# Router weights loaded third, value halves made with the keys', no sum begun where another ended, three row buffers, limits of one element

## The chip, the cores and the metric

The kernel runs on one core of a Trainium2 chip. The metric is the device time of one execution in microseconds. The engines are named as in the profile: PE (TensorE: matmuls; PEld its weight loads), DVE (VectorE), ACT (ScalarE), POOL (GpSimd) and SP (SyncE, which here issues the DMAs); a trailing q (SPq) is an engine's instruction queue. Each engine works through its own instructions in order and waits for the others by semaphores.

## What is computed

Thresholded attention over 2 batches, 8 heads, 576 positions and 64 elements a head (in each row of scores only those within tau of the row's maximum stay), then a feed-forward layer (512 to 2048 to 512, ELU), then a mixture of 8 experts, each token to its best one:

```python
scores = scale * q @ k.T
thresh = max(scores, axis=-1) - tau
scores = where(scores >= thresh, scores, -1e9)
attn = exp(scores - max(scores)); attn /= attn.sum(-1)
x = (attn @ v) as [1152 tokens, 512]
h = x @ w_in;  x = where(h > 0, h, exp(min(h, 0)) - 1) @ w_out
logits = x @ w_gate;  e = argmax(logits)        # at most 288 tokens for each expert
out = softmax(logits)[e] * (relu(x @ w1[e]) @ w2[e])
```

## The kernel before

The 1152 tokens make 9 tiles of 128. Operands of matmuls are split into two fp16 halves (a high one, and a low one made of the rest), and a product is three matmuls.

The first part is written out by hand, in steps i = 0 to 37 (`manual_schedule`): the order of the lines is each engine's order. A step is one pair of heads (j = i % 4) of one query tile (t = i // 4). The two score tiles of a step are already computed by PE at the end of the step before. In a step, in this order: PE multiplies the probabilities of step i - 2 with the values (`emit_pv`); SP issues loads (`load_k`, `load_v`, `load_q`); while keys are still to be prepared (i = 0 to 2 and 15 to 18), ACT copies the next pair's keys to fp16 (`prep_k`, first half, L216); `emit_max` takes on DVE both heads' maxima (L272) and then the two limits, nb for the exponential (L273) and th for the mask (L274), each as one instruction on two elements per partition; ACT makes both exponentials (L278); DVE makes the keys' low half (L218). In steps 0 to 16 conversions of the feed-forward weights follow (`conv`: three DVE instructions, L363, L364, L367, then two on ACT and one on POOL), one here and, from step 2 on, one more at the end of the step. DVE then masks each head with its sum (L284), PE computes the next step's scores (L250), ACT copies the probabilities to fp16 (L293), POOL makes their low half (L294) and SP transposes them by DMA (L299, tile pt). The end of the step holds `setup_rest` (in step 0), the values' halves (`prep_v`: ACT L107, DVE L108; steps 0 to 3 and 16 to 19), the q halves of the next tile (j = 2) and, in steps 14 to 19, one sixth each of the zero fill of the DRAM table disp (L180). `zero_out` writes zeros to the output in step 26.

Feed-forward work is put into the steps by `piece`, from step 7 on: three calls in steps 7 to 17 (FILL = 3), two afterwards. All but the last stand before the masks, as piece(2), and take only second-layer products (`mm2_chunk`, L423, 12 matmuls); the last stands at the end of the step, as piece(1), and takes a first-layer chunk (`mm1_chunk`, L391, 48 matmuls) where one is ready. Second-layer products of a tile are summed in one PSUM bank, mmb (one buffer). A sum of two products is emptied by ACT (L434, `acc`) and later added to by DVE (L437); a sum that ends at the fourth product starts the tile's routing. The emptying is written by `settle`, after the masks and the scores. What is left of the pieces when the steps are over runs in a loop of single pieces, whose instructions are not in an order written out by hand.

`route` copies a finished tile's row to a row buffer x2 (ACT L447 high half, DVE L452 low half; two buffers), transposes it by DMA, takes logits on PE, chooses and ranks on DVE, one tile at a time and a piece of it per step, and sends the rows into disp by an indirect DMA from POOL (L503). After the loop the last tile is routed; the transposed rows of expert 0 (xa, L596) are read for that. The experts follow, with weights loaded in 32 parts (stg).

## Time and profile before

| | us |
|---|---|
| runs of the kernel before | 601.43, 598.35, 595.74; median 598.35 |
| the profiled execution | 600.27 |
| its span, first to last instruction | 598.6 |
| busy: PE, DVE, ACT, POOL | 447.4 (75%), 415.7 (69%), 350.4 (59%), 268.6 (45%) |
| mean granted clock of PE, share of full speed | 0.912 |
| the steps (first to last maximum) | 10.3 to 357.5 |

All times of single instructions are from the one profiled execution, counted from its span's start. A busy share is a mean over parts with different limits. Where the profile names what an engine waited for, it is the last of its semaphores by the profile.

### The profile page before, as it was taken

What the parts mean: (1) busy time and instruction counts of PE and PEld (TensorE: products, weight loads), DVE (VectorE), ACT (ScalarE), POOL (GpSimd) and SP (SyncE); (2) the same over time, 40 slices, a digit from 0 to 9 for tenths busy, and PEclk for the clock granted to TensorE, in tenths of its full rate; (3) what the DMA queues carried; (4) which work ended last, traced back from release to release, by engine and by line L of the source; (5) the groups of instructions that cost most, each with busy time, mean ns of one, the idle gap of its engine ahead of it and who ended that gap; (6) DMA issues with size and microseconds to landing.
All of it is one profiled execution on the core that took longest, in us unless ns stands there. A gap on an engine that the chain in (4) does not pass through costs nothing.

```text
span 598.6 us, 13017 instructions
## 1 busy us (share of the span) xinstructions
PE 447.4 (75%) x5343; PEld 361.3 (60%) x5343; DVE 415.7 (69%) x768; ACT 350.4 (59%) x511; POOL 268.6 (45%) x195
## 2 busy tenths in 40 slices
PE   1124255855848799679799999998799998788792
PEld 0013134534616477547477776777789998787671
DVE  4488899999968868578888874687336566655530
ACT  4346568677765765355667554677266675665531
POOL 0326466765764353536356553432432541442242
PEclk9997667879979899979999999998899999798897
DMA  5645677678786858625765444777377998797621
GB/s 180 209 138 146 180 203 212 192 199 229 174 202 184 169 130 220 116 55 119 200 184 111 86 93 99 206 286 240 111 146 246 275 234 257 250 260 217 202 60 38
DMA packets 150771, 105.59 MB, mean 176 GB/s; under 512 B 135209, under 2 KB 135209, under 8 KB 146608
## 3 DMA queue, kind: packets, MB, share of 16 engines
q1 hardware_dynamic: 148064, 99.94, 63.1%
q0 software_dynamic: 2640, 4.74, 2.2%
q8 instruction: 44, 0.72, 0.5%
q14 instruction: 23, 0.19, 0.1%
HBM read 60.06 MB, written 12.68 MB: 122 GB/s over the span
## 4 chain that ended last, share of the span: by engine, by line
DVE 39%; DMA 21%; issue 12%; ACT 12%; PE 12%; POOL 2%; SPq 1%; DVEq 0%; POOLq 0%; ACTq 0%
DMA stg<-in_w_dram 9%; DVE m L272 6%; DVE pp L284 6%; PE mma L391 4%; DVE we L639 4%; PE mmb L423 4%; DMA yr<-yt 4%; DVE cvp L364 4%; DVE cvp L363 3%; ACT pp L278 3%; DMA out_dram<-y,ix 3%; ACT we L636 2%; DVE gf L408 2%; DVE nb L273 2%; DMA disp<-x,slot_i 2%
## 5 line engine op out<-in xcount | busy, mean ns | idle before, releaser
L250 PE MATMUL s<-kst,qst 128*128 128x288 f16 (+1 forms) x320 | 54.1, 330 | 91.6 <-DVE pp L284 82.1
L294 POOL TENSOR_TENSOR phl<-pp,phl 128x1152 f16<-128x1152 f32 x36 | 85.5, 2374 | 81.7 <-issue 73.7
L423 PE MATMUL mmb<-wo,g 128*128 128x512 f16 x384 | 96.3, 402 | 20.9 <-ACT acc L434 7.9
L391 PEld LDWEIGHTS <-wi 128*128 128x128 f16 x1728 | 103.5, 101 | 9.7 <-issue 6.9
L639 DVE SCALAR_TENSOR_TENSOR we<-stg,we 128x1024 f16<-128x1024 f32 x64 | 79.5, 1276 | 37.8 <-ACT we L636 37.5
L250 PEld LDWEIGHTS <-qst 128*128 128x128 f16 (+1 forms) x320 | 28.9, 110 | 115.0 <-DVE pp L284 68.3
L278 ACT ACTIVATE pp<-s,nb,escale 128x576 f32<-128x576 f32 x72 | 55.9, 826 | 66.7 <-DVE nb L273 56.7
L391 PE MATMUL mma<-xt,wi 128*128 128x128 f16 x1392 | 87.2, 225 | 4.7 <-DVE gf L408 4.6
L636 ACT ACTIVATE we<-stg 128x1024 f16<-128x1024 f32 x64 | 64.2, 1047 | 42.5 <-DMA stg<-in_w_dram 41.6
L676 PE MATMUL mm<-xs,we 128*128 128x196 f16 x768 | 73.9, 261 | 13.3 <-DVE g L759 5.0
L676 PEld LDWEIGHTS <-we 128*128 128x128 f16 x768 | 70.3, 104 | 15.8 <-DVE we L639 8.0
L423 PEld LDWEIGHTS <-g 128*128 128x128 f16 x384 | 37.0, 102 | 66.4 <-issue 29.5
L689 POOL TENSOR_TENSOR ht<-rf,ht 128x392 f16<-128x392 f32 x32 | 35.2, 1109 | 77.1 <-ACT ht L688 40.0
L284 DVE SCALAR_TENSOR_TENSOR pp<-s,th,pp 128x576 f32<-128x576 f32 x72 | 55.9, 814 | 11.0 <-ACT pp L278 10.2
L413 POOL TENSOR_TENSOR g<-gf,g 128x512 f16<-128x512 f32 x36 | 45.1, 1254 | 34.4 <-ACT g L412 34.3
L732 PE MATMUL mm<-ht,we 128*128 128x196 f16 x672 | 58.4, 248 | 1.6 <-DVE yt L743 1.6
L732 PEld LDWEIGHTS <-we 128*128 128x128 f16 x672 | 57.4, 98 | 1.8 <-issue 1.7
L272 DVE TENSOR_REDUCE m<-s 128x1 f32<-128x576 f32 x72 | 50.9, 747 | 6.4 <-PE s L250 6.4
L293 ACT ACTIVATE phl<-pp 128x1152 f16<-128x1152 f32 x36 | 41.7, 1157 | 8.4 <-DVE pp L284 8.3
L316 PE MATMUL pv<-vst,pt 128*128 128x64 f16 (+3 forms) x1080 | 45.0, 204 | 1.9 <-DVE xf L332 1.9
L316 PEld LDWEIGHTS <-pt 128*128 128x128 f16 (+1 forms) x1080 | 42.8, 106 | 3.8 <-issue 2.3
L376 POOL TENSOR_TENSOR wi<-cv,wi 128x512 f16<-128x512 f32 x16 | 18.5, 1158 | 55.1 <-ACT cv L375 55.1
(128 smaller groups left out, 635.7 us busy)
## 6 DMA issues: line engine op xcount, KB each, us to landing
stg<-in_w_dram SPq DMA_DIRECT2D x32, 1024.0 KB, 5.2
cst<-in_w_in_dram SPq DMA_DIRECT2D x16, 512.0 KB, 4.3
cst<-in_w_out_dram SPq DMA_DIRECT2D x16, 512.0 KB, 4.2
disp<-zero SPq DMA_DIRECT2D x6, 771.0 KB, 6.8
qraw<-in_qt_dram SPq DMA_DIRECT2D x9, 512.0 KB, 4.6
vraw<-in_vb_dram SPq DMA_DIRECT2D x8, 320.0 KB, 5.9
kraw<-in_kt_dram SPq DMA_DIRECT2D x8, 288.0 KB, 6.5
out_dram<-zero SPq DMA_DIRECT2D x1, 2304.0 KB
```

The costliest lines, as they stand in the source:

```text
L250: nc.tensor.matmul(s[a:z, half, 0:288], q2[:, pas, h, a:z], kst[b, h // 2][:, h % 2, half * 288:(half + 1) * 288], start=(pas == 0), stop= ...
L272: nc.vector.tensor_reduce(out=m[:, z:z + 1], in_=sc[z], axis=AX.XY, op=ALU.max)
L278: nc.scalar.activation(out=pp[:, z].rearrange("p (a c) -> p a c", a=2), in_=s, func=ACTF.Exp, bias=nb[:, z:z + 1], scale=escale,)
L284: nc.vector.scalar_tensor_tensor(out=e, in0=s, scalar=th[:, z:z + 1], in1=e, op0=ALU.is_ge, op1=ALU.mult, accum_out=rsum[t_][:, h:h + 1],)
L294: nc.gpsimd.tensor_tensor(out=d[:, 1], in0=flat, in1=d[:, 0], op=ALU.subtract)
L316: nc.tensor.matmul(o[a:e, h:h + w // D, :].rearrange("p h d -> p (h d)"), q[:, ph * 9 + blk, a:e], vt[:, vh, c:c + w], start=(blk == 4 and ...
L391: nc.tensor.matmul(ps[:, o * P:(o + 1) * P], w[:, wh, kk, :], xt[t_][:, xh * 4 + kk, :], start=(k_ == 0), stop=(k_ == 11),)
L423: nc.tensor.matmul(ps, gt[t_, q][:, gh, o, :], w[:, wh, :], start=(first and o == 0 and n == 0), stop=(last_ and o == QF - 1 and n == 2),)
L636: nc.scalar.activation(out=w[:, 0, part], in_=t[:, part], func=ACTF.Copy, scale=SC)
L639: nc.vector.scalar_tensor_tensor(out=w[:, 1, part], in0=t[:, part], scalar=SC, in1=w[:, 0, part], op0=ALU.mult, op1=ALU.subtract)
L676: nc.tensor.matmul(ps[:, o * n:(o + 1) * n], w[:, wh, kk % 2, f * P:(f + 1) * P], t[:, xh * 4 + kk, :], start=(k_ == 0), stop=(k_ == 11),)
L732: nc.tensor.matmul(ps[:, o * n:(o + 1) * n], w[:, wh, f % 4, j * P:(j + 1) * P], h2[:, gh, f, :], start=(f == 0 and n_ == 0), stop=(f == 7 ...
```

## The change

- The load of the router weights goes out third, after the first k and q loads. The set-up instructions of POOL stand at the very start (`setup_pool`); what is left of `setup_rest` runs at the end of step 1 instead of step 0.
- `prep_v` becomes a generator like `prep_k`: its ACT copy stands before the maxima and exponentials of the step, its DVE low half after the keys' low half, before the conversion.
- `emit_max` works on one head: maximum, nb, and then the exponential of that head; the th limits of both heads follow. m, nb and th are tiles of one element per partition (four small instructions a step in place of two).
- `pick2` returns nothing while a sum has ended that `settle` has not yet emptied.
- Three row buffers x2 instead of two.
- The zero parts run in steps 8 to 13; the zero tile has half a row (514 elements), so that the transfers' pieces are half as long and twice as many (1,028 B instead of 2,056 B for disp, 1,024 B instead of 2,048 B for the output).

```diff
--- before.py
+++ after.py
@@ -67,7 +67,7 @@
     QF = 4
     QG = 2
 
-    ZSTEP, ZPARTS, ZOUT = 14, 6, 26
+    ZSTEP, ZPARTS, ZOUT = 8, 6, 26
     zeroed = [False]
 
     cap = min(cap, NT)
@@ -134,7 +134,7 @@
     cum = const.tile([P, E], F16, name="cum")
     wg_f = const.tile([P, 4, E], F32, name="wg_f")
     wg = const.tile([P, 2, 4, E], F16, name="wg")
-    zero = const.tile([P, ROW], F16, name="zero")
+    zero = const.tile([P, ROW // 2], F16, name="zero")
     lnsc = const.tile([P, 1], F32, name="lnsc")
     eps = const.tile([P, 1], F32, name="eps")
     xsc = const.tile([P, 1], F32, name="xsc")
@@ -151,41 +151,42 @@
             out=cadd, in0=neg, scalar=-3.0e38, in1=cadd, op0=ALU.mult, op1=ALU.add
         )
 
-    def setup_rest():
-        nc.sync.dma_start(out=wg_f, in_=w_gate)
-        nc.scalar.activation(out=wg[:, 0], in_=wg_f, func=ACTF.Copy, scale=SC)
-        nc.vector.scalar_tensor_tensor(
-            out=wg[:, 1], in0=wg_f, scalar=SC, in1=wg[:, 0], op0=ALU.mult, op1=ALU.subtract
+    def setup_pool():
+        nc.gpsimd.iota(ev_i, pattern=[[1, E]], base=-E, channel_multiplier=0)
+        nc.gpsimd.iota(ids, pattern=[[P, NTILE]], base=0, channel_multiplier=1)
+        nc.gpsimd.memset(ones, 1.0)
+
+        nc.gpsimd.affine_select(
+            out=tri, in_=ones, pattern=[[1, P]], compare_op=ALU.is_gt, fill=0.0,
+            base=0, channel_multiplier=-1,
         )
         nc.gpsimd.memset(lnsc, LN_GS)
         nc.gpsimd.memset(eps, 1e-9)
         nc.gpsimd.memset(xsc, SC / XS)
         nc.gpsimd.memset(zero, 0.0)
         nc.gpsimd.memset(cum, 0.0)
-        nc.gpsimd.memset(ones, 1.0)
-        nc.gpsimd.iota(ev_i, pattern=[[1, E]], base=-E, channel_multiplier=0)
+
+    def setup_rest():
+        nc.scalar.activation(out=wg[:, 0], in_=wg_f, func=ACTF.Copy, scale=SC)
+        nc.vector.scalar_tensor_tensor(
+            out=wg[:, 1], in0=wg_f, scalar=SC, in1=wg[:, 0], op0=ALU.mult, op1=ALU.subtract
+        )
         nc.vector.tensor_copy(ev, ev_i)
-        nc.gpsimd.iota(ids, pattern=[[P, NTILE]], base=0, channel_multiplier=1)
         nc.vector.tensor_scalar(ids, ids, OOB_ID, None, ALU.bitwise_xor)
-
-        nc.gpsimd.affine_select(
-            out=tri, in_=ones, pattern=[[1, P]], compare_op=ALU.is_gt, fill=0.0,
-            base=0, channel_multiplier=-1,
-        )
 
     def zero_fill(part, parts):
         n = E * CS // P
         r0, r1 = part * n // parts, (part + 1) * n // parts
         if r0 < r1:
             nc.sync.dma_start(
-                out=disp.rearrange("(p r) c -> p r c", p=P)[:, r0:r1],
-                in_=zero.bitcast(U16).unsqueeze(1).to_broadcast([P, r1 - r0, ROW]),
+                out=disp.rearrange("(p r) (a c) -> p (r a) c", p=P, a=2)[:, 2 * r0:2 * r1],
+                in_=zero.bitcast(U16).unsqueeze(1).to_broadcast([P, 2 * (r1 - r0), ROW // 2]),
             )
 
     def zero_out():
         nc.sync.dma_start(
-            out=out.rearrange("(p r) c -> p r c", p=P),
-            in_=zero[:, 0:2 * DM].bitcast(F32).unsqueeze(1).to_broadcast([P, NTILE, DM]),
+            out=out.rearrange("(p r) (a c) -> p (r a) c", p=P, a=2),
+            in_=zero[:, 0:DM].bitcast(F32).unsqueeze(1).to_broadcast([P, 2 * NTILE, DM // 2]),
         )
 
 
@@ -223,7 +224,11 @@
     def prep_v(b, j):
         v1 = raw_t.pop(("v", b, j))
         vt = attn.tile([P, 2, VC], F16, name="vst", tag="vst", bufs=6)
-        split(vt[:, 0], vt[:, 1], v1, SC, "dve")
+        nc.scalar.activation(out=vt[:, 0], in_=v1, func=ACTF.Copy, scale=SC)
+        yield
+        nc.vector.scalar_tensor_tensor(
+            out=vt[:, 1], in0=v1, scalar=SC, in1=vt[:, 0], op0=ALU.mult, op1=ALU.subtract
+        )
         vst[b, j] = vt
 
     def prep_q(t_):
@@ -263,26 +268,27 @@
     pv_ps = {}
     xt = {}
 
-    def emit_max(sc):
-
-        m = attn.tile([P, 2], F32, name="m", tag="m")
-        nb = attn.tile([P, 2], F32, name="nb", tag="nb")
-        th = attn.tile([P, 2], F32, name="th", tag="th")
-        for z in range(2):
-            nc.vector.tensor_reduce(out=m[:, z:z + 1], in_=sc[z], axis=AX.XY, op=ALU.max)
+    def emit_max(s):
+        m = attn.tile([P, 1], F32, name="m", tag="m", bufs=2)
+        nb = attn.tile([P, 1], F32, name="nb", tag="nb", bufs=2)
+        nc.vector.tensor_reduce(out=m, in_=s, axis=AX.XY, op=ALU.max)
         nc.vector.tensor_scalar(nb, m, cmul, None, ALU.mult)
+        return m, nb
+
+    def emit_thr(m):
+        th = attn.tile([P, 1], F32, name="th", tag="th", bufs=2)
         nc.vector.tensor_scalar(th, m, cadd, None, ALU.add)
-        return nb, th
+        return th
 
     def emit_exp(s, nb, pp, z):
         nc.scalar.activation(
-            out=pp[:, z].rearrange("p (a c) -> p a c", a=2), in_=s, func=ACTF.Exp, bias=nb[:, z:z + 1], scale=escale,
+            out=pp[:, z].rearrange("p (a c) -> p a c", a=2), in_=s, func=ACTF.Exp, bias=nb, scale=escale,
         )
 
     def emit_mask(s, th, pp, z, t_, h):
         e = pp[:, z].rearrange("p (a c) -> p a c", a=2)
         nc.vector.scalar_tensor_tensor(
-            out=e, in0=s, scalar=th[:, z:z + 1], in1=e, op0=ALU.is_ge, op1=ALU.mult,
+            out=e, in0=s, scalar=th, in1=e, op0=ALU.is_ge, op1=ALU.mult,
             accum_out=rsum[t_][:, h:h + 1],
         )
 
@@ -443,7 +449,7 @@
         return shared.tile([P, c], dt, name=n, tag=n)
 
     def x2_hi(ps):
-        row = shared.tile([P, ROW], U16, name="x2", tag="x2", bufs=2)
+        row = shared.tile([P, ROW], U16, name="x2", tag="x2", bufs=3)
         nc.scalar.activation(out=row.bitcast(F16)[:, 0:DM], in_=ps, func=ACTF.Copy, scale=1.0 / GS)
         return row
 
@@ -542,7 +548,7 @@
     def last_block(j):
         if j == 0:
             last["x2t"] = eA.tile([P, 2, 4, P], F16, name="x2tl", tag="x2tl", bufs=1)
-            last["row"] = shared.tile([P, ROW], U16, name="x2", tag="x2", bufs=2)
+            last["row"] = shared.tile([P, ROW], U16, name="x2", tag="x2", bufs=3)
         ps = ps_e.tile([P, 512], F32, name="mm", tag="mm")[:, 0:P]
         for f in range(NF1):
             w = w1st["o", f]
@@ -810,6 +816,9 @@
         return None
 
     def pick2():
+        if done:
+
+            return None
         if summing:
             t_, q1 = summing
             q = nq2[t_]
@@ -875,8 +884,11 @@
 
     with tc.manual_schedule():
         setup_first()
-        for c in "kqkcvcvcc":
-            if c == "k":
+        setup_pool()
+        for c in "kqgkcvcvcc":
+            if c == "g":
+                nc.sync.dma_start(out=wg_f, in_=w_gate)
+            elif c == "k":
                 load_k(0, len([1 for x in raw_t if x[0] == "k"]))
             elif c == "q":
                 load_q(0)
@@ -910,6 +922,8 @@
                 if 0 <= jk < NPAIR:
                     halves.append(prep_k(b, jk))
                 jv = i - base
+                if 0 <= jv < NPAIR:
+                    halves.append(prep_v(b, jv))
                 if 0 <= jv + 1 < NPAIR and (b or jv >= 1):
                     load_v(b, jv + 1)
             if on and j == 0 and t_ + 1 < NTILE:
@@ -917,9 +931,12 @@
             for g in halves:
                 next(g)
             if on:
-                lim = emit_max(sc)
+                th = []
                 for z in range(2):
-                    emit_exp(sc[z], lim[0], pair_p[i], z)
+                    m, nb = emit_max(sc[z])
+                    emit_exp(sc[z], nb, pair_p[i], z)
+                    th.append(m)
+                th = [emit_thr(m) for m in th]
             for g in halves:
                 next(g, None)
             flush(1)
@@ -929,7 +946,7 @@
                 piece(2)
             if on:
                 for z in range(2):
-                    emit_mask(sc[z], lim[1], pair_p[i], z, t_, 2 * j + z)
+                    emit_mask(sc[z], th[z], pair_p[i], z, t_, 2 * j + z)
                     if i + 1 < NSTEP:
                         sc[z] = emit_s((i + 1) // NPAIR, (2 * i + 2 + z) % H)
                 emit_split(i)
@@ -939,16 +956,13 @@
             if i >= LAG and (i - LAG) % NPAIR == NPAIR - 1:
                 emit_x((i - LAG) // NPAIR)
                 x_at[(i - LAG) // NPAIR] = i
-            if i == 0:
+            if i == 1:
                 setup_rest()
             for _ in range(nc_ - 1):
                 conv_next()
             slot()
             if nf:
                 piece(1)
-            for b, base in ((0, 0), (1, 4 * NPAIR)):
-                if 0 <= i - base < NPAIR:
-                    prep_v(b, i - base)
             if on and j == 2 and t_ + 1 < NTILE:
                 prep_q(t_ + 1)
             if ZSTEP <= i < ZSTEP + ZPARTS:
```

## Rows read from the trace of the kernel before

**Rows 1.** Windows: us; busy PE, PEld, DVE, ACT, POOL; clock, DMA share, GB/s

```profile
62.00:162.40 100.40, 58.56 (x666) 43.76 (x667) 98.08 (x169) 67.50 (x98) 60.90 (x42) 0.76 0.76 204
257.00:366.00 109.00, 99.54 (x1273) 73.13 (x1272) 88.21 (x197) 66.75 (x95) 58.13 (x36) 0.97 0.52 122
```

**Rows 2.** Timeline, steps 0, 1: start, us, engine, line, operation [idle before <-releaser]

```profile
9.17 0.43 SPq L204 DMA_DIRECT2D vraw<-in_vb_dram  x1
17.14 0.81 DVE L284 SCALAR_TENSOR_TENSOR pp<-s,th,pp 128x576 f32<-128x576 f32 x1
23.86 0.57 SPq L155 DMA_DIRECT2D wg_f<-in_w_gate_dram  x1
26.00 0.23 ACT L156 ACTIVATE wg<-wg_f 128x32 f16<-128x32 f32 x1 [6.84 <-DMA wg_f<-in_w_gate_dram]
26.89 0.83 DVE L108 SCALAR_TENSOR_TENSOR vst<-vraw,vst 128x640 f16<-128x640 f32 x1 [0.28 <-ACT vst L107]
27.63 1.41 DVE L272 TENSOR_REDUCE m<-s 128x1 f32<-128x576 f32 x2
```

**Rows 3.** Groups by line: count, busy us, mean ns, idle before

```profile
L108 DVE SCALAR_TENSOR_TENSOR vst<-vraw,vst 128x640 f16<-128x640 f32 x8 | 12.2, 1524 | 8.9 <-ACT vst L107 8.9
L364 DVE SCALAR_TENSOR_TENSOR cvp<-cst,cvp 128x512 int32<-128x512 int32 x32 | 22.3, 696 | 1.1
```

**Rows 4.** One line, all 36 steps: duration ns min/median/max, first and last start

```profile
L273 DVE TENSOR_SCALAR nb<-m,cmul x36: 228/303/2177, 12.0 to 357.6; 128x2 f32<-128x2 f32 x36
```

**Rows 5.** Windows of L273 alone, then of L274: us, DVE busy us (count)

```profile
62.00:162.40 100.40, 5.56 (x11) 0.76 0.76 204
62.00:162.40 100.40, 11.23 (x11) 0.76 0.76 204
```

**Rows 6.** Timeline: limits of two elements and of one beside POOL

```profile
71.66 1.20 DVE L274 TENSOR_SCALAR th<-m,cadd 128x2 f32<-128x2 f32 x1
71.69 1.15 POOL L376 TENSOR_TENSOR wo<-cv,wo 128x512 f16<-128x512 f32 x1
278.54 2.37 POOL L294 TENSOR_TENSOR phl<-pp,phl 128x1152 f16<-128x1152 f32 x1 [3.02 <-issue]
279.47 0.15 DVE L488 TENSOR_SCALAR over<-pos 128x1 f32<-128x1 f32 x1
```

**Rows 7.** Timeline, steps 15 to 18: PE and DVE

```profile
175.17 4.60 PE L423 MATMUL mmb<-wo,g 128*128 128x512 f16 x12 [7.93 <-ACT acc L434]
180.42 0.76 DVE L272 TENSOR_REDUCE m<-s 128x1 f32<-128x576 f32 x1 [4.85 <-PE s L250]
198.75 4.44 PE L423 MATMUL mmb<-wo,g 128*128 128x512 f16 x12 [4.25 <-DVE acc L437]
```

**Rows 8.** Timeline, steps 22 and 23: ACT and PE

```profile
254.86 0.60 ACT L447 ACTIVATE x<-mmb 128x512 f16<-128x512 f32 x1 [8.98 <-DMA disp<-x,slot_i]
256.24 2.29 PE L423 MATMUL mmb<-wo,g 128*128 128x512 f16 x5 [6.42 <-DVE x L452]
```

**Rows 9.** Timeline after the attention: PE

```profile
401.50 2.75 PE L423 MATMUL mmb<-wo,g 128*128 128x512 f16 x12
428.85 1.47 PE L596 MATMUL mm<-xa,ident 128*128 128x196 f16 x8 [2.05 <-DMA xa<-disp]
```

**Rows 10.** DMA view: queue (packets, MB, share), issues (KB, us to landing)

```profile
q1 hardware_dynamic: 148064, 99.94, 63.1%
disp<-zero SPq DMA_DIRECT2D x6, 771.0 KB, 6.8
vraw<-in_vb_dram SPq DMA_DIRECT2D x8, 320.0 KB, 5.9
pt<-phl SPq DMA_TRANSPOSE x36, 3.9
```

**Rows 11.** Timeline, steps 8 to 10: a transpose and its use

```profile
106.86 1.96 SPq L299 DMA_TRANSPOSE pt<-phl  x1
114.61 1.03 PE L316 MATMUL pv<-vst,pt 128*128 128x128 f16 x27 [1.28 <-DVE xf L332]
```

## The prediction

> **What bounds the kernel now.** I read the windows view first, because the attention part has no single bound. In steps 4 to 14 the vector engine is busy 98.08 of 100.40 us while TensorE has 58.56 [rows 1]: whatever takes time out of VectorE's queue there shortens the step. From step 24 to the end of the attention it is the other way round: PE is busy 99.54 of 109.00 us and VectorE 88.21 [rows 1], so VectorE's time is worth little, and only what lets PE stand still counts. Then I read the timeline at the places where both are idle. There are four. (1) Between steps 0 and 1 nothing runs on VectorE from 17.95 (the last mask, 17.14 + 0.81) until after 26.00: ScalarE stands 6.84 us at the copy of the router weights, whose transfer SyncE issued only at 23.86, behind step 0's transpose [rows 2]. (2) In step 15 a sum of the second layer ends and another begins in the one bank mmb; its first product waits 7.93 us for ScalarE to empty the bank, the scores of step 16 stand behind it in PE's order, and VectorE waits 4.85 us for them. The same pattern in step 17 costs PE 4.25 us [rows 7]. (3) In step 22 ScalarE waits 8.98 us for a row buffer that the first indirect transfer to disp still holds, and PE 6.42 us behind it [rows 8]. (4) All along, the two small instructions of a step, L273 and its twin L274, are stretched: L273 takes up to 2.18 us where its shortest is 0.23 [rows 4]; the timeline shows such a long one ending with GpSimd's subtraction beside it (71.66 + 1.20 against 71.69 + 1.15) [rows 6].
>
> **The change part by part.** The sum is made against the profiled execution, 600.27 us (span 598.6); the median of the three runs, 598.35, lies 1.9 below it.
>
> *Router weights third, the rest of the set-up in step 1, GpSimd's part first.* The load goes out while SyncE would wait for a buffer of the next k load anyway, and GpSimd is idle at the start, so both are free. The wait of 6.84 us on ScalarE goes. What is late next: the value halves now stand ahead of step 0's exponentials. The first v load is issued at 9.17 and a v load lands in 5.9 us, so at 15.1; the copy (taken as long as the low half) and the low half follow, 0.83 us each, then the conversion (three instructions of 0.70) and the masks (two of 0.81). Step 0's masks end near 20.5 instead of 17.95, and step 1's maximum starts near 20.6 instead of 27.63 [rows 2, 3, 10]. I take -7.0 (bounds -6, and -9.7 if v costs nothing there).
>
> *Value halves with the keys'.* Eight low halves take 12.2 us where the one at 26.89 takes 0.83, so 5.6 us of their time is a hold, and VectorE idles 8.9 us ahead of them [rows 2, 3]. 14.5 us at most could go, some 7 in steps 1 to 3. Against it: the two copies now stand ahead of the exponentials on ScalarE, the keys' low half, which also reads two tensors of SBUF, now meets GpSimd's subtraction in place of the values' half, and in step 3 the values' copy stands behind the q copies of step 2's end. Walking the three steps with these orders I get -2, less 0.5 for the three small set-up instructions that now run in step 1 (0.15 each by L488): -1.5 (bounds +1 and -5). The four halves of steps 16 to 19 are in the next term.
>
> *Limits of one element, one head at a time.* In steps 4 to 14 the two instructions take 5.56 + 11.23 us [rows 5]; eleven times two of 0.23 [rows 4] is 5.0. The excess is 11.8 us, in VectorE's full queue. Does an instruction on one element per partition wait too? L488 is the same operation on 128x1, started at 279.47 inside a subtraction of GpSimd that runs from 278.54 to 280.91, and took 0.15 us [rows 6]: it did not wait. Two more instructions per step cost at most 2 x 0.15 us by L488 and nothing if they overlap their neighbours; half of that, 11 x 0.15 = 1.7, comes back. -10.1 (bounds -12 and, if GpSimd's hold moves to the next instruction with two tensors, -5). That the first exponential starts a maximum earlier (about 0.7 us, half of the 1.41 of [rows 2]) helps nothing here, since a conversion keeps VectorE busy meanwhile.
> The rule that speaks against this: the Trainium skill, VectorE: DVE Perf Modes, What auto-detection actually checks, lets a one-source instruction in SBUF take the mode that uses both ports where the outer dimensions are both even or equal; source and destination of one element are equal, so by its letter the hold would stay. By that rule this term is +1.7 and not -10.1; L488 speaks against it.
>
> *No sum begun where another ended.* Followed through the steps, the piece lists let the condition bite exactly twice, in steps 15 and 17, the two waits of (2). The scores no longer stand behind them. At least VectorE's 4.85 goes, at most both waits of PE, 4.85 + 4.25 = 9.1. In step 16 to 18 the k and v halves take some of it back as above. -7.
>
> *Three row buffers.* With three, the third tile needs no row back, and by the piece lists the fourth asks for one in step 27, five steps after the first transfer went out in step 22. PE's 6.42 goes, and about 1.2 us of products that ran at the lower clock after the stand (4.44 to 4.60 us for twelve against 2.75 [rows 7, 9]). -7.6 (bounds -6 and -9).
>
> *Steps 24 to 35.* PE idles 109.00 - 99.54 = 9.5 us [rows 1], mostly at the scores and at a bank that VectorE has still to empty; both come earlier when limits don't wait and exponentials start a maximum earlier. I take half: -4.6 (bounds 0 and -9.5).
>
> *What is paid.* The piece lists put 55 products in place of 56 into the attention; the missing one is run after it, where PE is the bound: +2.75 [rows 9]. There the last token tile but one is also summed two places later, and the xa load, for which PE waits 2.05 us already [rows 9], hangs on its routing: +1.5 (bounds 0 and 5).
> The zero parts move from steps 14 to 19, where no wait on them shows, into steps 8 to 13. Their pieces halve, to 1,028 B; no packet between 512 B and 2 KB is in this trace. Bounds: the queue spent 63.1% of 598.6 us on 16 engines, 6,043 engine-us, on 148,064 packets and 99.94 MB [rows 10], 41 ns a packet or 60 us a MB. A part (0.79 MB, 768 packets) is 2.0 us by packets, 3.0 by bytes, 5.0 by both. A step of steps 4 to 14 lasts 9.13 us at a DMA share of 0.76 [rows 1], 6.9 us of work; shortened to 8.2 it leaves 1.3. Six parts at 3.0 overload the queue by 6 x 1.7 = 10 us. What is late first is the transposed pt: it has 7.75 us from issue to use [rows 11] and lands in 3.9 [rows 10], so 3.9 is spare, and PE idles (100.40 - 58.56) / 11 = 3.8 us a step there [rows 1], which takes a late product up. About 10 - 8 = 2 to 3 is left: +3 (bounds 0 and 6 x 3.7 - 8 = 14).
>
> Sum: -7.0 - 1.5 - 10.1 - 7 - 7.6 - 4.6 + 2.75 + 1.5 + 3 = -30.55, so 569.7 for an execution like the profiled one and 567.8 for the median. I predict **567.8 us**. The second mixture of experts is untouched.
>
> **The rivals.** *A, the zero parts set the pace of steps 8 to 13.* For it: the share of 0.76 leaves little. Against: the slack above. At the price by both, +14 instead of +3: 579; with pt's slack gone as well (22): 587.
> *B, the limits wait as before.* The change then doesn't do what it says: -10.1 turns into +1.7 and a third of the -4.6 falls, 567.8 + 11.8 + 1.5 = 581. L488 speaks against it; for it, only that it is one row. (The Trainium skill's rule named above, on VectorE: DVE Perf Modes, would have it so.)
> *C, slower.* Zero pieces cost by count and not by bytes. Today's part lands in 6.8 us [rows 10]; twice the pieces at the same price each is 13.6, an overload of 6 x 12.3 - 8 = 66 us in place of 3: 631. It decides from about 8.3 us a part: 6 x (8.3 - 1.3) - 8 = 34 eats the gain of 34 that stands without this term. Against: 13.6 us is 283 ns a packet, and the mean of all is 41.
> *D, more than the sum.* Both waits of PE go whole (-2.1), the v halves' holds go (-3.5), the idle of steps 24 to 35 goes whole (-5), the zero parts hide (-3): 554.
>
> **How the numbers follow.** Forecast (556 to 579) 0.64; A (579 to 590) 0.13; B 0.07; C 0.04; D (below 556) 0.09; about no change, several terms at their low ends together, 0.03. About 1% is what a measurement here can tell from no change, 592.4 to 604.3 on the median. Faster: forecast, A, B, D, 0.92 (0.01 of A kept for its far end); same 0.04; slower 0.04. The range reaches from half of D to most of A: 554 to 586, with about 0.85 inside; the forecast's own is 556 to 579.
>
> **What would show it.** L156 on ScalarE without a wait, and the second pair of maxima near 20.5. Limits of 0.15 us each, beside GpSimd's work too; if they still reach 1 to 2 us, B. No L423 that waits for L434 or L437, no L447 that waits for disp. Steps 4 to 14 near 8.2 us each, at a DMA share near 0.9 in 8 to 13; if PE's products with vst wait there for pt, or VectorE for cst, A or C. PE after step 18 busy above 95%. What would make the prediction wrong beyond that: a wait of the first exponentials on v longer than 2.4 us, or a stretch after the attention that grows by more than the 4.25.

## The result and the profile after

The changed kernel takes 569.09 us (median of 4 runs, 568.14 to 572.67) where the kernel before, measured beside it, takes 597.33 (595.74 to 601.43): ratio 0.953, 95% interval 0.946 to 0.959. The forecast was 567.8, the range 554 to 586. Its profiled execution has a span of 570.6 us.

The experiments below were measured later, in three sets on three chips; the kernel before took 597.82, 598.52 and 597.77 us (medians) there, so medians of different sets can be compared to about 1 us. One run of the experiment with one-element limits alone (585.49 us, at a granted clock of 0.895) fell in a slower state of the chip and is left out of its figures.

The page of the profile after, its first, second and third parts (engines, DMA packets, the main queue):

```profile
PE 438.8 (77%) x5343; PEld 360.5 (63%) x5343; DVE 400.1 (70%) x840; ACT 351.1 (62%) x511; POOL 266.8 (47%) x195
DMA packets 154227, 105.59 MB, mean 185 GB/s; under 512 B 135209, under 2 KB 142121, under 8 KB 150064
...
q1 hardware_dynamic: 151520, 99.94, 70.9%
```

The queue moves the same megabytes as in [rows 10] in 3,456 packets more, which are the halved zero pieces (2,304 of them in the six parts for disp, 1,152 in the output's). Its share is 70.9% of 570.6 us where it was 63.1% of 598.6: 405 us instead of 378. The halved pieces explain little of these 27 us. The kernel before with halved, early parts (an experiment below) has a share of 63.4% of 603.5 us, which is 383. A larger piece, 15 us, comes with the third row buffer, as the experiment with two buffers shows.

Where the 28 us went is read best from the start of each step's first maximum in the timeline. This table is worked out from those starts (lengths in us; the last two rows go on to the first product of the first expert, L676 before and L682 after, and to the end of the span). "Limits alone" and "late zeros" are experiments below, "forecast" puts the prediction's terms in their stretches.

```
                   before  limits alone   after   late zeros   after - before   forecast
start to step 1     27.63      28.06       20.53     20.55         -7.10          -7.0
steps 1 to 3        35.07      34.33       34.02     34.31         -1.05          -1.5
steps 4 to 13       90.62      82.74       84.15     83.80         -6.47        } -7.1
step 14              9.26       8.01       11.57      8.26         +2.31        }
step 15             17.84      17.49       23.68     12.90         +5.84        } -7.0
steps 16 to 21      59.30      57.58       55.44     56.85         -3.86        }
step 22             16.38      15.40        7.58      7.58         -8.80          -7.6
step 23             10.16       8.07        9.14      9.15         -1.02
steps 24 to 34      89.86      81.93       79.93     80.06         -9.93          -4.6
to the first expert 76.2       77.2        80.1      78.5          +3.9           +4.25
the experts        166.3      164.7       164.5     165.6          -1.8
```

The experts' part is the same code in all kernels of this document, and its stretch takes 160.7 to 166.3 us in their fourteen traces, so the last row can't be told from scatter.

The total fits, the middle does not: at the start of step 24 the prediction stood at -30.2, the trace at -20.2. Two places carry this: step 15, which is 5.84 us longer where a wait was to go, and the steps from 24 on, which gained twice the term. First the start, as the timeline after has it:

```profile
14.91 0.74 ACT L227 ACTIVATE vst<-vraw 128x640 f16<-128x640 f32 x1 [1.85 <-DMA vraw<-in_vb_dram]
...
19.21 0.81 DVE L290 SCALAR_TENSOR_TENSOR pp<-s,th,pp 128x576 f32<-128x576 f32 x1
...
20.53 0.76 DVE L274 TENSOR_REDUCE m<-s 128x1 f32<-128x576 f32 x1 [0.50 <-PE s L255]
...
30.55 2.37 POOL L300 TENSOR_TENSOR phl<-pp,phl 128x1152 f16<-128x1152 f32 x1 [0.39 <-ACT phl L299]
30.62 2.34 DVE L171 SCALAR_TENSOR_TENSOR wg<-wg_f,wg 128x32 f16<-128x32 f32 x1 [1.35 <-ACT wg L170]
```

The wait of 6.84 us of [rows 2] is gone, v lands at 14.9, the masks end at 20.0 and step 1's maximum starts at 20.53, all as forecast. The last two rows are a cost that was not: the router's low half, moved into step 1, runs beside GpSimd's subtraction and ends with it.

The limits, all of the attention, from the view of the tiles nb and th (minimum / median / maximum in ns), to be read against [rows 4]:

```profile
L275 DVE TENSOR_SCALAR nb<-m,cmul x72: 212/214/215, 11.1 to 327.7; 128x1 f32<-128x1 f32 x72
L280 DVE TENSOR_SCALAR th<-m,cadd x72: 202/204/207, 12.2 to 328.0; 128x1 f32<-128x1 f32 x72
```

Not one of the 144 waits. The new stall comes next, in the timeline after (SPq is SyncE's queue of DMA issues; a row's second number is how long the issue held it):

```profile
144.32 8.64 SPq L305 DMA_TRANSPOSE pt<-phl  x1
...
155.43 0.42 SPq L181 DMA_DIRECT2D disp<-zero  x1
...
155.90 0.54 SPq L200 DMA_DIRECT2D kraw<-in_kt_dram  x1
...
165.17 1.16 ACT L217 ACTIVATE kst<-kraw 64x1152 f16<-64x1152 f32 x1 [12.40 <-DMA kraw<-in_kt_dram]
...
166.37 1.35 DVE L219 SCALAR_TENSOR_TENSOR kst<-kraw,kst 64x1152 f16<-64x1152 f32 x1 [13.94 <-ACT kst L217]
```

Step 15 begins at 150.27, and ScalarE stands 12.40 us for the first k load of the second batch. That load belongs to step 14, which began at 138.70, and is issued 17.2 us later, right behind the sixth zero part. In the kernel before it went out 4.7 us into its step (which began at 153.32), and nothing waited for it:

```profile
157.99 0.51 SPq L199 DMA_DIRECT2D kraw<-in_kt_dram  x1
...
165.73 1.15 ACT L216 ACTIVATE kst<-kraw 64x1152 f16<-64x1152 f32 x1
```

SyncE is late because the issues of a transposed pt, for steps 9 to 14, hold it for 5.0 to 8.64 us each, where the median of the kernel before is 1.95. The windows view after, steps 8 to 12 and step 13 (us; busy us of PE, PEld, DVE, ACT, POOL; clock; DMA share; GB/s):

```profile
87.20:129.10 41.90, 31.09 (x382) 23.57 (x380) 40.43 (x87) 32.27 (x48) 28.79 (x20) 0.89 1.03 241
129.10:138.70 9.60, 5.04 (x64) 4.19 (x62) 9.25 (x21) 7.24 (x11) 7.46 (x6) 0.82 1.16 229
```

The DMA share adds up the times of all packets over the 16 engines, so it can pass 1. It does so through the steps that carry the parts, and the waits view after (total us, times, longest) adds that PE's products with pt waited too:

```profile
ACT kst L217 <- DMA kraw<-in_kt_dram: 21.4, 5, 12.4
...
PE pv L322 <- DMA pt<-phl: 12.4, 5, 4.6
```

PE waited 4.56 us of this in step 13, 4.10 in step 14 and 2.39 in step 15. In step 14 VectorE also waited for loads of feed-forward weights (cst), 1.82 and 0.58 us.

### The profile page after: what moved, and what is told of

Its sections match the earlier page's. It is cut to its first block, busy times and chain, and to the rows that moved or that the text cites. A ratio compares the mean times of both kernels' runs of the same rounds, so it can differ in the third digit from the quotient of the medians.

```text
span 570.6 us, 13138 instructions
## 1 busy us (share of the span) xinstructions
PE 438.8 (77%) x5343; PEld 360.5 (63%) x5343; DVE 400.1 (70%) x840; ACT 351.1 (62%) x511; POOL 266.8 (47%) x195
## 3 DMA queue, kind: packets, MB, share of 16 engines
q1 hardware_dynamic: 151520, 99.94, 70.9%
## 4 chain that ended last, share of the span: by engine, by line
PE 26%; DMA 26%; DVE 25%; ACT 10%; issue 9%; POOL 2%; SPq 1%; POOLq 0%; DVEq 0%; ACTq 0%
PE mma L397 9%; DMA stg<-in_w_dram 9%; PE mmb L429 6%; DMA out_dram<-y,ix 5%; DMA kraw<-in_kt_dram 4%; DVE pp L290 4%; PE s L255 3%; DVE we L645 3%; ACT we L642 3%; DVE cvp L370 3%; PE pv L322 3%; DVE m L274 3%; DMA yr<-yt 3%; DVE cvp L369 3%; PE mm L682 2%
## 5 line engine op out<-in xcount | busy, mean ns | idle before, releaser
L300 POOL TENSOR_TENSOR phl<-pp,phl 128x1152 f16<-128x1152 f32 x36 | 85.4, 2373 | 63.1 <-issue 45.1
L255 PEld LDWEIGHTS <-qst 128*128 128x128 f16 (+1 forms) x320 | 30.3, 114 | 104.4 <-DVE pp L290 50.7
L429 PE MATMUL mmb<-wo,g 128*128 128x512 f16 x384 | 89.7, 382 | 1.9 <-POOL g L419 1.8
L682 PE MATMUL mm<-xs,we 128*128 128x196 f16 x768 | 72.9, 259 | 13.4 <-DVE we L645 4.6
L682 PEld LDWEIGHTS <-we 128*128 128x128 f16 x768 | 69.4, 103 | 15.9 <-DVE we L645 9.6
L284 ACT ACTIVATE pp<-s,nb,escale 128x576 f32<-128x576 f32 x72 | 58.4, 827 | 24.7 <-DVE nb L275 10.4
L429 PEld LDWEIGHTS <-g 128*128 128x128 f16 x384 | 35.4, 98 | 41.1 <-POOL g L419 3.4
L738 PEld LDWEIGHTS <-we 128*128 128x128 f16 x672 | 56.9, 97 | 1.6 <-issue 1.6
L274 DVE TENSOR_REDUCE m<-s 128x1 f32<-128x576 f32 x72 | 53.8, 748 | 2.1 <-PE s L255 2.1
L322 PEld LDWEIGHTS <-pt 128*128 128x128 f16 (+1 forms) x1080 | 43.6, 107 | 17.2 <-DMA pt<-phl 14.0
```

The lines of the kernel that those rows point to most:

```text
L255: nc.tensor.matmul(s[a:z, half, 0:288], q2[:, pas, h, a:z], kst[b, h // 2][:, h % 2, half * 288:(half + 1) * 288], start=(pas == 0), stop= ...
L274: nc.vector.tensor_reduce(out=m, in_=s, axis=AX.XY, op=ALU.max)
L284: nc.scalar.activation(out=pp[:, z].rearrange("p (a c) -> p a c", a=2), in_=s, func=ACTF.Exp, bias=nb, scale=escale,)
L300: nc.gpsimd.tensor_tensor(out=d[:, 1], in0=flat, in1=d[:, 0], op=ALU.subtract)
L322: nc.tensor.matmul(o[a:e, h:h + w // D, :].rearrange("p h d -> p (h d)"), q[:, ph * 9 + blk, a:e], vt[:, vh, c:c + w], start=(blk == 4 and ...
L429: nc.tensor.matmul(ps, gt[t_, q][:, gh, o, :], w[:, wh, :], start=(first and o == 0 and n == 0), stop=(last_ and o == QF - 1 and n == 2),)
```

## The experiments

**Zero parts late again.**

```diff
-    ZSTEP, ZPARTS, ZOUT = 8, 6, 26
+    ZSTEP, ZPARTS, ZOUT = 14, 6, 26
```

> The changed kernel with one number undone: the six zero parts go out in steps 14 to 19 again, not 8 to 13 (pieces stay halved). Theory Q (backlog): in steps 8 to 13 the transfers ask for more than the queue gives (share 1.06 over these steps), the backlog is passed on, and it ends as the one wait of 12.40 us on the k load in step 15, with 12.4 us of waits for pt on PE before it. Then the wait of step 15 falls under 2 us, steps 10 to 14 lose 2 to 4 us, steps 15 to 19 get 2 to 5 slower by the parts beside the k and v loads: 555 to 562 us. Rival K: the k load is late for another reason (it shares two buffers with the q loads and stands behind a transpose on its queue): the wait stays at 10 us or more, 566 to 572. Rival S (the parts only move the collision): the k and v loads of steps 16 to 19 wait by as much instead, 565 to 572, with the long wait in another step.

Measured: 559.19 us (555.89 to 560.0), 9.9 below the changed kernel; ratio to the kernel before 0.933 [0.927, 0.940]. Its timeline, in the same place:

```profile
138.48 2.73 SPq L305 DMA_TRANSPOSE pt<-phl  x1
...
143.70 0.51 SPq L200 DMA_DIRECT2D kraw<-in_kt_dram  x1
...
150.07 1.15 ACT L217 ACTIVATE kst<-kraw 64x1152 f16<-64x1152 f32 x1
...
195.50 0.74 ACT L227 ACTIVATE vst<-vraw 128x640 f16<-128x640 f32 x1 [3.43 <-DMA vraw<-in_vb_dram]
```

The issue of pt is back at 2.73 us, the k load goes out 5.0 us into its step and nothing waits for it. That is theory Q: step 14 takes 8.26 us in place of 11.57 and step 15 12.90 in place of 23.68. K falls. Of S one piece is left: ScalarE waits 3.43 us for a v load beside a part in step 19, which is 1.4 us longer. Late, the parts stand behind all the cst loads, of which the last (L360) goes out at 151.44 here and the first part at 152.04. The spans differ by 13.0 us, the medians by 9.9.

**The same parts in the kernel before.** The old kernel with `ZSTEP` 8 and the halved zero row, as in the diff of the change.

> The kernel before with the zero parts of the changed kernel: steps 8 to 13, pieces of 1028 B. Theory R (the price hangs on the length of the steps: at 9.1 us a step with a share of 0.71 the parts find room, and what is late falls into the wait for the bank in step 15): 595 to 602 us, the wait on the k load in step 15 under 5 us. Rival T (the parts cost 10 us wherever they stand): 604 to 610, with a wait of 8 us or more on the k load.

Measured: 603.58 us (600.77 to 606.02), ratio 1.0083 [1.0052, 1.0114]: 5.8 us slower. The timeline:

```profile
153.79 8.63 SPq L299 DMA_TRANSPOSE pt<-phl  x1
...
164.94 0.55 SPq L199 DMA_DIRECT2D kraw<-in_kt_dram  x1
...
174.24 1.16 ACT L216 ACTIVATE kst<-kraw 64x1152 f16<-64x1152 f32 x1 [8.37 <-DMA kraw<-in_kt_dram]
```

Steps 8 to 14 keep their length to 0.02 us in total; only step 15 grows, from 17.84 to 25.22. The time lies just over R's range and under T's. The slower kernel pays 5.8 us and the quicker one 9.9, which would fit R's idea that the price hangs on the steps' length, but the quicker kernel also has the third row buffer and its longer issues (next experiment), so this is not shown. R's bound on the wait (under 5 us) is broken at 8.37, which is nearer to T. That steps 8 to 14 are unharmed and the stall comes later, behind SyncE, is what the prediction had wrong.

**Two row buffers.**

```diff
-        row = shared.tile([P, ROW], U16, name="x2", tag="x2", bufs=3)
+        row = shared.tile([P, ROW], U16, name="x2", tag="x2", bufs=2)
```

(in both places where the row buffer is made)

> The changed kernel with two row buffers in place of three. Theory of the prediction: the third token tile asks for a row that the first indirect transfer still holds, ScalarE waits some 9 us for disp again and PE some 6 behind it: 575 to 579 us. Rival: the rule that no sum begins where another ended has already moved the routings one step apart (steps 17, 19 and 23 in place of 17, 18 and 22), so that the row is free in time: within 2 us of the changed kernel, 567 to 571.

Measured: 565.99 us (564.23 to 568.6). Step 22 takes 7.58 us with two buffers as with three, and ScalarE does not wait for disp (VectorE does once, for 0.5 us). The routing argument of the rival is right, and the third buffer bought nothing here. It even cost something: the time is 3 us lower without it, of which the trace has 0.5 at the start and 2.7 in steps 14 and 15. The views of tile pt, first of the changed kernel and then of this one, show where that may come from (ns, minimum / median / maximum; then the us to landing):

```profile
L305 SPq DMA_TRANSPOSE pt<-phl x36: 2422/2800/8637, 23.7 to 333.7; - x36
DMA to landing us min/median/max: 4.6/5.5/11.4
...
L305 SPq DMA_TRANSPOSE pt<-phl x36: 1740/1970/8585, 23.2 to 330.4; - x36
DMA to landing us min/median/max: 3.9/4.3/11.5
```

With three row buffers each issue of pt holds SyncE for 0.8 us longer and lands 1.2 us later, and the queue is busy 68.9% of 564.9 us here, 389 us, against 405. All fourteen traces agree: the median issue is 2.72 to 2.80 us in the six kernels with three row buffers and 1.95 to 2.03 in the eight with two. Another pair below (late_sum_after_sum and late_sum_two_buffers) differs in the buffer alone as well, 2.76 against 1.98. That the buffer lengthens the issue is therefore shown. Why it does (where it puts the other tiles in SBUF, for one) is not, nor that the 3 us are this and nothing else.

**Whole zero rows, at two buffers.** The halved row makes the room for the third buffer; with two, the whole one fits.

```diff
-    zero = const.tile([P, ROW // 2], F16, name="zero")
+    zero = const.tile([P, ROW], F16, name="zero")
...
-                out=disp.rearrange("(p r) (a c) -> p (r a) c", p=P, a=2)[:, 2 * r0:2 * r1],
-                in_=zero.bitcast(U16).unsqueeze(1).to_broadcast([P, 2 * (r1 - r0), ROW // 2]),
+                out=disp.rearrange("(p r) c -> p r c", p=P)[:, r0:r1],
+                in_=zero.bitcast(U16).unsqueeze(1).to_broadcast([P, r1 - r0, ROW]),
```

(and the same in `zero_out`)

> The changed kernel with two row buffers (the whole zero row needs the space) and zero pieces of a whole row, 2056 B, in steps 8 to 13; to be read against two_buffers, which differs in the pieces alone. Theory by bytes: the parts move the same bytes, the share of steps 8 to 13 stays above 1, and the time is within 2 us of two_buffers. Theory by count: with half the packets a part lands in 6 to 7 us in place of 8.0, the wait on the k load in step 15 falls from 12.4 to under 5 us, and the time is 6 to 10 us below two_buffers.

Measured: 561.23 us (557.46 to 561.43), 4.8 below two_buffers. A part lands in 6.0 us where it took 7.7; step 14 is 8.25 us in place of 10.86 and step 15 17.88 in place of 21.68, with 5.8 us of wait on the k load where two_buffers has 11.2. This lies between the two theories. Bytes alone don't price a part, and count alone doesn't either, since 5.0 us of the stall of step 15 stay (17.88 against 12.90 with late parts).

**Limits on two elements in the changed kernel.** Both maxima, then nb and th of two elements, then the exponentials, as before.

> The changed kernel with the limits of a step on two elements again, both maxima first, as before. Theory V (VectorE is the bound of steps 4 to 14): each of the two instructions reaches 1 to 2.2 us again, steps 4 to 14 grow by 0.7 to 1 us each, and the time is 577 to 583 us. Rival Q2 (the zero parts are the bound of steps 8 to 15): the instructions are as long, but the backlog drains in the longer steps and the wait of step 15 shrinks by as much, so only steps 4 to 7 and those after 18 pay: 569 to 575.

Measured: 579.96 us (578.6 to 581.57), 10.9 above the changed kernel. Steps 4 to 13 take 91.67 us (0.75 more each), steps 24 to 34 85.68 (5.75 more). The sum is theory V's, but steps 14 and 15 are 2.3 and 2.5 us shorter, as Q2 has it. The edit also puts both maxima ahead of the exponentials again; what the order of one head at a time is worth by itself was not run.

**One-element limits alone, in the kernel before.**

```diff
-        nc.vector.tensor_scalar(nb, m, cmul, None, ALU.mult)
-        nc.vector.tensor_scalar(th, m, cadd, None, ALU.add)
+        for z in range(2):
+            nc.vector.tensor_scalar(nb[:, z:z + 1], m[:, z:z + 1], cmul, None, ALU.mult)
+        for z in range(2):
+            nc.vector.tensor_scalar(th[:, z:z + 1], m[:, z:z + 1], cadd, None, ALU.add)
```

> The kernel before with the two limits computed on one element each, four instructions where there were two, and nothing else. Theory of the prediction: none waits for GpSimd, steps 4 to 14 lose 0.7 to 0.9 us each, the steps after 24 some 3 to 5 us in all: 584 to 589 us, each limit 0.15 to 0.25 us. Rival B: one element waits as two do, and there are more of them: 598 to 606. Rival F: the hold moves on to the next instruction that has two operands in SBUF: limits of 0.2 us, but longer conversions, and 594 to 599.

Measured: 577.51 us (576.51 to 577.53), ratio 0.965 [0.957, 0.973]: 21.0 us of the 28 by these four lines, more than any theory gave. The limits take 196 to 213 ns, so B falls. The conversions are as long as before (66.4 us for VectorE's 96 instructions of them in both traces), so F falls too. The table says where the time went: 7.9 us in steps 4 to 13 and 1.3 in step 14, near the forecast, but also 5.1 in steps 15 to 23 and 7.9 in steps 24 to 34. The windows of L273 and then L274 in the kernel before, for steps 15 to 23 and 24 to 35:

```profile
162.58:266.26 103.68, 6.21 (x9) 0.92 0.65 153
266.26:366.00 99.74, 9.21 (x12) 0.98 0.55 131
...
162.58:266.26 103.68, 3.93 (x9) 0.92 0.65 153
266.26:366.00 99.74, 7.54 (x12) 0.98 0.55 131
```

At 0.23 us each these would be 4.1 and 5.5 us, so 6.0 and 11.2 us were holds there too. The prediction had priced none of it as such: steps 15 to 23 got no term, and from 24 on "VectorE's time is worth little". The windows of steps 24 to 34, first of the kernel before and then of this one, show what PE made of it:

```profile
266.26:356.12 89.86, 82.97 (x1083) 61.96 (x1081) 73.80 (x165) 56.27 (x80) 47.98 (x30) 0.98 0.56 135
...
251.68:333.61 81.93, 79.67 (x1078) 60.73 (x1076) 63.93 (x188) 56.07 (x80) 48.00 (x30) 1.00 0.67 149
```

PE's idle time falls from 6.9 to 2.3 us, and its busy time falls as well, from 82.97 to 79.67, at a granted clock of 1.00 in place of 0.98.

**Two-element limits with the zero parts late.** The two edits above together.

> late_zeros (559.19) with limits on two elements, both maxima first. In the changed kernel the same edit cost 10.9 us, alone it gained 21.0 on the kernel before. Theory M (the zero parts' backlog hid part of it: in the longer steps the queue drained, step 15 was 2.5 and step 14 2.3 us shorter): here it costs more, 573 to 580 us, steps 4 to 13 0.75 us longer each and steps 14 and 15 not shorter. Rival N (what it gained on the kernel before beyond 11 us went with the other edits): 568 to 572.

Measured: 572.32 us (569.83 to 575.88), 13.1 above late_zeros, just under M's range and over N's. Steps 4 to 13 cost 0.79 us each, step 14 takes 9.27 us (8.26 in late_zeros) and step 15 the same 12.9. Without the backlog nothing is handed back in steps 14 and 15, which is M. The price does not reach the 21 us of the edit alone, so part of N holds too. The two profiled executions lie further apart than the medians, 16.4 us at step 35 and 16.6 at the end of the span.

**Sums after sums, with the zero parts late.**

```diff
     def pick2():
-        if done:
-
-            return None
         if summing:
```

> late_zeros (559.19) with the rule that no sum begins where another ended taken out; three row buffers stay. Prediction's theory: PE waits 4 to 8 us at the bank in steps 15 and 17 again, and the routings move back to steps 17, 18 and 22, but the third buffer keeps ScalarE from waiting for disp: 564 to 568, step 15 some 5 us longer, step 22 at 7.6. Rival D (the third buffer does nothing, it was the order of the routings): step 22 is 16 us again: 572 to 577. Rival E (without the zero parts' backlog the bank is emptied in time): within 2 us of late_zeros.

Measured: 560.95 us (557.15 to 562.87), which late_zeros' 559.19 can't be told from. The time is E's and not the theory's 564 to 568, but E's reason is wrong, for the attention shows the wait: PE stands 7.93 us at the bank, step 15 takes 18.48 us (12.90 in late_zeros), and step 35 starts 6.05 us later. Then the stretch to the first expert is 74.7 us in place of 78.5, as if the product that the rule pushes out of the attention were paid behind it. Step 22 is 8.74 us, so D falls.

**The same with two row buffers.**

> late_zeros with both edits undone: sums may follow one another, and two row buffers. If either edit alone cures the wait of step 22, it is back here alone: step 22 at 15 to 17 us and 572 to 577 us. If the wait was the zero parts' or the transfers' place and not the buffers': step 22 stays near 8 and the time is that of late_sum_after_sum.

Measured: 567.7 us (567.18 to 568.27), 6.75 above late_sum_after_sum and 8.5 above late_zeros; the expectation was 572 to 577. Step 22 is 15.50 us, as it had it, and the timeline has [rows 7] and [rows 8] again:

```profile
158.89 5.28 PE L429 MATMUL mmb<-wo,g 128*128 128x512 f16 x12 [7.94 <-ACT acc L440]
...
236.07 0.60 ACT L453 ACTIVATE x<-mmb 128x512 f16<-128x512 f32 x1 [8.05 <-DMA disp<-x,slot_i]
```

So either edit alone takes the wait for disp away, and only the rule takes the wait at the bank away as well. The stretch to the first expert is 78.3 us here, without the rule as with it (78.5), so the 74.7 of the run before is no measure of what the rule costs behind the attention.

**Value halves at the end of the step, with the zero parts late.** `prep_v` is run where it was before, its two instructions in a row.

> late_zeros with the value halves at the end of a step, one after another, as before (the rest of the set-up stays in step 1). Theory of the prediction: step 1 begins some 2.4 us earlier, since no copy waits for v ahead of the first exponentials, and steps 1 to 3 and 16 to 19 give it back with holds and waits of the low halves: within 3 us of late_zeros, 557 to 562. Rival G (the halves' place is worth their whole 14 us): 566 to 572. Rival H (the new place costs more than it saves): 553 to 556.

Measured: 559.71 us (556.53 to 562.43), late_zeros' time, as forecast. But step 1 begins at 21.89 us, 1.3 later and not 2.4 earlier: the masks of step 0 do end earlier, but the low half behind them takes 2.46 us beside GpSimd's subtraction. Step 35 starts 3.15 us later and the span ends 2.8 later, of which the medians show 0.5. The two times can't be told apart, so G and H fall.

**The set-up's order alone, in the kernel before.** `setup_pool`, the load third, `setup_rest` at the end of step 1.

> The kernel before with the set-up of the changed kernel alone: GpSimd's part first, router weights loaded third, the rest at the end of step 1. Theory of the prediction: 6.84 us on ScalarE go, without a v copy ahead of the exponentials step 1 begins 7 to 9 us earlier, and nothing later waits for longer: 588 to 592 us. Rival U (a later wait, of the bank in step 15 or of the row in step 22, swallows it): 596 or more.

Measured: 593.03 us (590.81 to 594.94), ratio 0.993 [0.989, 0.997], a gain of 4.7 us and one short of the theory's range. Step 1 begins at 22.29 us, 5.3 earlier and not 7 to 9; step 35 starts 4.8 earlier. No later wait swallows it, so U falls. The other 1.8 us of the changed kernel's start came with its other edits, 1.3 of them with the place of the value halves by the experiment before this one.

**A version from these.** Late zero parts in whole rows, two row buffers, `if i == 17: setup_rest()`.

> late_zeros with zero pieces of a whole row, two row buffers (the whole zero row takes the space of the third) and the rest of the set-up in step 17 in place of 1. Theory: the third buffer isn't needed while no sum follows another; the router's low half took 2.34 us in step 1 beside GpSimd's subtraction and stretched a step that VectorE bounds, where step 17 has room: step 1 some 2.5 us shorter, the rest as in late_zeros, 554 to 558 us. Rival W (step 22 waits for disp again or the low half is in the way in step 17): 560 to 566.

Measured: 556.53 us (555.03 to 557.57), ratio 0.929 [0.926, 0.933]: below the changed kernel by 12.6 us, and below late_zeros by 2.7, with runs that overlap. The theory's range holds, and what each of the three edits on late_zeros is worth was not separated. Step 1 takes 10.00 us in place of 12.79, step 17 13.33 in place of 11.10: most of what the move gained early it paid there, where the low half took 0.58 us and the cast behind it 1.17. Two buffers do no harm (step 22 takes 7.75 us).

## Why the prediction came out, point by point

- **Set-up, -7.0.** Right in sum: step 1 starts at 20.53 us, forecast 20.6. The walk's split was wrong. It had the value halves ahead of the exponentials cost 2.7 us of a gain of 9.7; the set-up alone gives 5.3, and with the halves back at the end of step 0 the changed kernel with late parts starts step 1 later, not earlier.
- **Value halves, -1.5.** Near: -1.05 in steps 1 to 3. Its allowance of 0.5 us for the moved set-up instructions was mis-sized: it priced by L488 an instruction with two inputs in SBUF, which took 2.34.
- **Limits, -10.1 in steps 4 to 14.** Mechanism and size right: -9.1 alone, at 0.20 to 0.21 us a limit where 0.15 was forecast. The one row of L488 pointed the right way for one element with one input. B had a chance of 0.07 and is shown wrong.
- **Steps 24 to 35, -4.6.** The size failed: -9.93 up to step 34, over the bound of 9.5 taken from PE's idle time. "I take half" had no row behind it, and the bound held PE's busy time fixed, which fell too (by 3.3 us with the limits alone, which give 7.9 there in all). PE being the bound did not make the holds free. The likely way is that a limit stands between a maximum and its exponential, and the next scores, in PE's order, behind the masks. After the change PE is busy 88.31 of the 89.89 us from 246.11 on.
- **No sum begun, -7, and +4.25 paid.** The first size holds: -6.05 to step 35, with the zero parts late. What is paid behind the attention is not settled: +3.9 in this pair of runs, +0.2 against late_sum_two_buffers. In time the rule is nothing that can be told from no change, as long as there are three row buffers.
- **Three row buffers, -7.6.** The wait is real and goes: step 22 is 8.80 us shorter, and where the rule is absent the buffer is worth 6.75 us. But the buffer isn't what takes it away here. The rule does so already, since it moves the second and third routing from steps 18 and 22 to 19 and 23. Each edit was followed on the old order, not on the order that the other leaves. The total isn't hurt by this, for the wait stands in the sum once. For both edits together the net forecast was -10.35; undoing both costs 8.5. That the buffer lengthens every issue of pt was not foreseen.
- **Zero parts, +3 (0 to 14).** The step that failed: they cost 9.9. The prediction took 8 off an overload of 10 us, because what is late first, pt, had slack and PE had idle time to take it up. As far as step 13 that is so: steps 4 to 13 are only 0.35 us longer than with late parts, though PE waits for pt. What the prediction left out is the issuer. The issues of pt for steps 9 to 14 take 5.0 to 8.64 us in place of 2.7 to 3.5 with late parts, so that all loads behind them in SyncE's order are late together, and one of them, the k load that step 15 needs, has no slack. Steps 14 and 15 pay for it. No run measures the overload of 10 us by itself. Rival A's price, +14, is nearer than +3, but its place, steps 8 to 13, is not where the time went. Of C the direction is shown, 4.8 us for the larger count of packets, and not the size.

That the total is so near is luck. Steps 4 to 21 gained 12 us less than forecast, 10 of them by the zero parts, and steps 22 to 34 gained 7.6 us more, mostly through holds of VectorE that the prediction had not priced; the experts' scatter adds 1.8. What was to show the prediction wrong did show: steps 4 to 14 last 8.70 us and not 8.2, at a share of 1.03 and more in steps 8 to 13, with PE waiting for pt and VectorE for cst.

## What to carry to other kernels

Price a hold wherever it stands on the chain of a step, not only where its engine is full: one-element limits alone were worth 21 of 28 us, and in their trace 13 us went in steps 15 to 34, outside the stretch that showed them best. When two edits answer the same wait, follow the second on the order that the first leaves. And bulk transfers on a shared queue were paid here by the load that had no slack, some steps later: look at how long each issue holds the issuing engine, not at the share of bytes alone.

## What the runs showed of the hardware

One element does not always escape. In the trace after, an instruction on 128x1 with two inputs in SBUF does wait beside GpSimd's subtraction (256.44 + 2.38 = 258.82 against 257.58 + 1.25 = 258.83), where its median is 0.218 us; a one-input instruction on eight elements takes 2.23 us beside another such subtraction:

```profile
220.95 2.37 POOL L300 TENSOR_TENSOR phl<-pp,phl 128x1152 f16<-128x1152 f32 x1 [4.17 <-issue]
...
221.12 2.23 DVE L472 TENSOR_SCALAR oh<-ev,amin 128x8 f16<-128x8 f32 x1
...
256.44 2.38 POOL L300 TENSOR_TENSOR phl<-pp,phl 128x1152 f16<-128x1152 f32 x1 [1.57 <-issue]
...
257.58 1.25 DVE L495 SCALAR_TENSOR_TENSOR slot_f<-pos,slot_f,over 128x1 f32<-128x1 f32 x1
```

The Trainium skill, SBUF — State Buffer, Who interferes with whom, says that a VectorE instruction with two SBUF inputs contends with a GpSimd instruction that reads SBUF; L495 and L171 agree. The Trainium skill, VectorE: DVE Perf Modes, What auto-detection actually checks, gives the mode with both ports to a one-source instruction in SBUF whose outermost non-unit dimensions are both even or equal. One element has no such dimension, so the sentence does not settle its case; read as the prediction read it, as equal, the limits of one element would wait too. The 144 limits of 202 to 215 ns did not, and the measurement decides.

The issue of a DMA transpose (pt) lengthens from a median of 1.95 us in the kernel before to as much as 8.64 beside the early zero parts. That it comes with the parts is shown by taking them away and by putting them into the kernel before. A high share of the queue alone is not the sign of it: with late parts the share is 1.04 in step 14 and 1.02 in step 15, and the issues there take 2.7 to 3.3 us. What inside the queue holds the issuer is not shown. Apart from the zero parts, the third row buffer lengthens the median issue from 1.97 to 2.80 us.
